# Spectral mixing and Strassen MLP on one core: weight-block sums moved from GpSimd to accumulating DMAs, and a new order of VectorE's work

## The chip, the core and the metric

The kernel runs on one core of one Trainium2 chip. The metric is device time in microseconds (us): the median of three runs of the whole program. The engines are named as in the profile: PE is TensorE (its weight loads are listed apart as PEld), DVE is VectorE, ACT is ScalarE, POOL is GpSimd, SP is SyncE, which issues DMAs.

## What is computed

```python
h  = x + irfft2(rfft2(layernorm(x)) * (w_r + 1j * w_i))       # x: 1 x 2048 x 576
h2 = h + relu(layernorm(h) @ w1) @ w2                         # w1: 576 x 4608, w2: 4608 x 576
```

All inputs and the output are float32. The sizes are S = 2048 tokens, D = 576 and Dff = 4608.

## The kernel before, in words

**Stages.** The two Fourier transforms are done as matrix products with constant tables (forward up to about 65 us, the product with the filter up to about 115 us, the inverse from there on). The inverse transform runs in the loop over t = 0 to 22 near the end of the function: `inv_d(t)` and `inv_a(t)` handle token tile t (16 tiles), `stat2` and `norm2` apply the second layer norm, `sumsx` and `project` transpose the normed tokens and split each number into a high and a low float32r part. Tokens of tiles 0 to 7 land in `T` in SBUF, those of tiles 8 to 15 go through the DRAM tile `Td` and are fetched later.

**The MLP** uses a Strassen-like scheme with seven products instead of eight, in both of its matrix products, and each product is three float32r matmuls (high by high, high by low, low by high). It is cut into NS = 18 steps: steps 0 to 8 serve the first half of the tokens, steps 9 to 17 the second half, and each step handles 512 of the 4608 hidden columns. A step has 14 slots, k = 0 to 13: two units u of seven products m. `slot(S, k)` interleaves two steps: the first matrix product of step S (`mm1`, `evac`) and the second one of step S-1 (`form`, `prod`). Step 0's first product has no partner and is interleaved with the last tiles of the inverse transform (t = 16 to 22); step 17's second product runs alone at the end.

**Weight operands.** For w1, unit v = 2S+u needs 17 blocks of 128 columns in `WF` (high and low): four plain blocks, four sums S1 to S4 of blocks (two 128-row parts each) and the rows 512 to 575. `load1` fetches the plain blocks, `sums1` (L475) forms the sums on GpSimd into the buffer SW, `split1` (L483) makes high and low parts on ACT and DVE in four groups. For w2, `load2` fetches the blocks B11, B12, B21, B22 of a step, `sums2` (L493) forms T1 to T4 on GpSimd, partly in place, and `split2` (L504) makes the seven operands' high and low parts.

**Hidden operands.** `evac` (L541) adds the PSUM tiles X and Y and applies the relu; `hsum` (L513) forms sums of the hidden blocks on DVE; `form` (L520) makes high and low parts of them. `prod` (L555) does 12 matmuls and then adds the PSUM result to the token tile `xs` on DVE (L570).

**Order.** Nothing is reordered by a scheduler: each engine runs its instructions in the order in which the code records them, and semaphores between engines come from the tiles that are read and written. So on GpSimd a sum stands where `tasks_old`, `tasks_new`, `sums1` or the loop over t put it, and everything recorded behind it on GpSimd waits for it: L396 of `inv_d`, L223 to L226 of the layer norm, L423 of `sumsx`. The same holds for SP and its loads. The places of the sums before the change:

```python
if t in (0, 1, 4, 5):
    sums1(t // 4, t % 4)                                  # loop over t
...
if k == 11:
    split2(s, "B11")
    sums2("T1", "T2", "T3")                               # tasks_new
...
if v and k in (3, 5, 9, 12):
    sums1(v + 1, int(k in (5, 12)))
```

The functions that the change touches, as they stood:

## Time and profile before

| | |
|---|---|
| median of 3 runs | 1077.87 us (1076.83 to 1078.52) |
| the profiled execution | 1077.19 us; span of its instructions 1075.4 us |
| granted TensorE clock, mean | 0.99 |
| busy, share of the span | PE 94%, PEld 83%, DVE 86%, ACT 48%, POOL 34% |
| DMA | 85.13 MB, mean 79 GB/s |
| stages | from 243 us to 1043 us steps 1 to 17; before that the transforms and step 0, behind it the last second product |

A profile page counts an engine as busy while an instruction of its executes; a wait is put down to the instruction of another engine that ended it ("<-"). In rows of the timeline the columns are start, duration, engine, line, operation, what is written from what is read, shapes and count, and in brackets the idle time before and its releaser. A line is that of the kernel before; L161 is the helper that all ACT copies go through, L158 that of the transforms' matmuls, L467 the subtraction in `split`.

### The profile page before, as it was taken

Reading aid. Unit: us, or ns where it says so; the run is one execution under the profiler, and the core shown is the slowest. Engines: PE = TensorE matmul, PEld = TensorE weight load, DVE = VectorE, ACT = ScalarE, POOL = GpSimd, SP = SyncE. Lnnn points to the kernel's source line nnn. Section 1 sums busy time; section 2 is a strip of 40 time slices with the busy share of each in tenths; the row PEclk is TensorE's granted clock in tenths of the full one; section 3 lists DMA queues with packets and bytes.
Section 4 is the critical chain, followed back from the end, with each engine's and each line's share of the span. In section 5 each row is a group of like instructions: output and inputs, shape, how many; then the busy total and the mean of one; then the engine's idle time right before and its main releaser. Section 6 shows DMA issues by size and latency. Waiting matters only on the chain.

```text
span 1075.4 us, 16681 instructions
## 1 busy us (share of the span) xinstructions
PE 1011.2 (94%) x6344; PEld 887.4 (83%) x6344; DVE 921.2 (86%) x1367; ACT 514.9 (48%) x904; POOL 368.4 (34%) x384
## 2 busy tenths in 40 slices
PE   8999598779999999999999999999999999999997
PEld 7788476659988988888888989888898988888896
DVE  7587478679899898989989898998989898998987
ACT  4533133556464545545454544545454554545442
POOL 4200166453424252342425235242523424251420
PEclk9999899999999999999999999999999999999999
DMA  8850900563121212112121744212121121212013
GB/s 235 198 133 2 225 1 1 146 183 97 53 67 35 69 36 58 58 44 75 36 69 36 265 147 103 82 36 69 36 58 49 46 82 38 69 30 64 15 31 89
DMA packets 73936, 85.13 MB, mean 79 GB/s; under 512 B 5248, under 2 KB 69248, under 8 KB 72960
## 3 DMA queue, kind: packets, MB, share of 16 engines
q1 hardware_dynamic: 73856, 84.06, 27.7%
q8 instruction: 50, 0.82, 0.3%
q14 instruction: 30, 0.25, 0.1%
HBM read 71.98 MB, written 12.06 MB: 78 GB/s over the span
## 4 chain that ended last, share of the span: by engine, by line
PE 56%; DVE 30%; ACT 7%; issue 3%; DMA 2%; POOL 2%; SPq 1%; POOLq 0%; DVEq 0%; ACTq 0%
PE d L565 22%; PE X L539 15%; PE Y L539 9%; PE d L158 6%; DVE WF L467 6%; DVE e L467 5%; DVE A L570 4%; DVE G L467 3%; DVE h L516 3%; PE dd L158 2%; DVE HF L467 2%; DVE h L552 2%; ACT e L161 1%; ACT WF L161 1%; DVE st L220 1%
## 5 line engine op out<-in xcount | busy, mean ns | idle before, releaser
L539 PE MATMUL X<-T,WF 128*128 128x512 f32 x864 | 230.4, 399 | 12.1 <-DVE WF L467 8.8
L570 DVE TENSOR_TENSOR A<-A,d 128x576 f32<-128x576 f32 x252 | 188.2, 747 | 41.5 <-PE d L565 41.3
L565 PEld LDWEIGHTS d<-e,G 128*128 128x128 f32 x1512 | 213.7, 188 | 11.8 <-issue 1.4
L565 PE MATMUL d<-e,G 128*128 128x288 f32 x1512 | 221.2, 295 | 1.2 <-DVE A L570 1.0
L553 ACT ACTIVATE h<-h 128x512 f32<-128x512 f32 x108 | 68.3, 633 | 315.1 <-DVE h L552 314.7
L481 POOL TENSOR_TENSOR e<-e 128x256 f32<-128x256 f32 (+1 forms) x108 | 98.2, 916 | 300.0 <-DVE WF L467 289.2
L539 PEld LDWEIGHTS X<-T,WF 128*128 128x128 f32 x864 | 154.8, 190 | 44.5 <-DVE WF L467 15.8
L539 PE MATMUL Y<-T,WF 128*128 128x512 f32 x648 | 169.0, 396 | 15.5 <-DVE h L552 15.5
L467 DVE TENSOR_TENSOR WF<-e,WF 128x640 fp32r<-128x640 f32 (+2 forms) x144 | 142.4, 1000 | 32.5 <-ACT WF L161 32.5
L539 PEld LDWEIGHTS Y<-T,WF 128*128 128x128 f32 x648 | 115.4, 188 | 38.6 <-DVE h L552 19.5
L565 PEld LDWEIGHTS d<-e,e 128*128 128x128 f32 x756 | 106.9, 188 | 7.4 <-issue 1.8
L565 PE MATMUL d<-e,e 128*128 128x288 f32 x756 | 110.9, 295 | 1.8 <-DVE A L570 1.6
L565 PEld LDWEIGHTS d<-e,HF 128*128 128x128 f32 x756 | 107.7, 189 | 5.3
L565 PE MATMUL d<-e,HF 128*128 128x288 f32 x756 | 111.2, 296 | 0.0
L497 POOL TENSOR_TENSOR e<-e 128x576 f32<-128x576 f32 x18 | 32.3, 1796 | 229.6 <-DVE e L467 216.9
L467 DVE TENSOR_TENSOR e<-e,e 128x576 fp32r<-128x576 f32 x108 | 96.6, 908 | 15.7 <-ACT e L161 14.4
L516 DVE TENSOR_TENSOR h<-h,h 128x512 f32<-128x512 f32 (+1 forms) x126 | 109.8, 882 | 0.0
L467 DVE TENSOR_TENSOR G<-h,G 128x512 fp32r<-128x512 f32 x126 | 103.6, 823 | 0.1
L161 ACT ACTIVATE WF<-e 128x640 fp32r<-128x640 f32 (+2 forms) x144 | 91.0, 645 | 9.1 <-POOL e L481 9.1
L481 POOL TENSOR_TENSOR e<-e,e 128x256 f32<-128x256 f32 x72 | 82.0, 1139 | 2.8
L161 ACT ACTIVATE u<-X 128x512 f32<-128x512 f32 x72 | 42.5, 590 | 82.4 <-PE X L539 82.3
L161 ACT ACTIVATE G<-h 128x512 fp32r<-128x512 f32 x126 | 77.8, 619 | 6.5 <-DVE h L516 3.5
(103 smaller groups left out, 1296.4 us busy)
## 6 DMA issues: line engine op xcount, KB each, us to landing
e<-in_B_w_dram SPq DMA_DIRECT2D x72, 288.0 KB, 2.9
e<-in_B_w_dram SPq DMA_DIRECT2D x36, 512.0 KB, 3.7
Td<-h SPq DMA_DIRECT2D x28, 256.0 KB, 3.0
T<-Td SPq DMA_DIRECT2D x7, 1024.0 KB, 8.8
A<-in_A_x_dram SPq DMA_DIRECT2D x16, 288.0 KB, 9.2
e<-in_B_w_dram SPq DMA_DIRECT2D x72, 64.0 KB, 3.4
out_dram<-A SPq DMA_DIRECT2D x32, 144.0 KB, 2.5
X<-in_A_x_dram SPq DMA_DIRECT2D x12, 288.0 KB, 7.7
```

Of the source, the lines that this page charges most:

```text
L158: nc.tensor.matmul(o, l, r, start=start, stop=stop)
L161: nc.scalar.activation(o, i, AF.Copy, **kw)
L220: nc.vector.bn_stats(st[:, i, h, :], xs[:, t0 + i, 288 * h:288 * h + 288])
L467: nc.vector.tensor_sub(l, v, h)
L481: (nc.gpsimd.tensor_sub if n_ else nc.gpsimd.tensor_add)(*ops[n_])
L497: nc.gpsimd.tensor_sub(d, a, b)
L516: f(raw(s, d, j), raw(s, a, j), raw(s, b, j))
L539: nc.tensor.matmul(o, l, r, start=first and n_ == 0, stop=n_ == len(ops) - 1, skip_group_check=not first)
L552: nc.vector.tensor_add(h, a, Y)
L553: nc.scalar.activation(h, h, AF.Relu)
L565: nc.tensor.matmul(o[:, tt], f[:, l, j, 128 * tt:128 * tt + 128], w[:, r, j], start=first and n_ == 0, stop=n_ == 5, skip_group_check=not ...
L570: nc.vector.tensor_add(xt, xt, o)
```

## The change

Four things are changed at once.

1. **Sums of w1's blocks.** `sums1` is gone but for one 128-column sum (`rsum`). `wsum(v, step)` builds S1 to S4 in four steps per unit: step 0 is a plain load from SP of the block A21 into four places; steps 1 to 3 are DMAs from GpSimd's queue with `accum_op=ALU.add`, which add A22 to three of them, A11 to three and A12 to one. Each step is two DMAs. SW has two buffers now instead of one, so a unit's sums are started up to two units ahead.
2. **Sums of w2's blocks.** `sums2` is gone. Each operand is loaded by SP from its first block, and the others are added by GpSimd's accumulating DMAs: T2 takes two, T1 and T3 one each, T4 three. B11, B21 and B22 are plain loads. Operands rotate through five buffers.
3. **Signs.** The seven products are turned so that all weight sums are plain sums: S1, S2 and the A22 blocks are split with the factor -1 (on DVE a `scalar_tensor_tensor` in place of the subtraction), two relu evacuations take scale -1, two `hsum`s change sign, and P6 and P7 are subtracted from the tokens instead of added.
4. **Order and buffers.** `total` (the addition to the tokens) is cut out of `prod`; for odd k it stands before `tasks_new`, for even k behind `tasks_late`. Splits are spread over the slots, `hsum` of S2 and S4 is done in one instruction instead of two, `split1` has five groups instead of four. The `Td` stores are issued right behind each split and their staging tiles are apart from the hidden tiles (`HF`, 4 buffers; `h` has 6 instead of 7).

The core of the diff:

```diff
-    def sums1(v, part, only=None):
...
+    def wsum(v, step):
+        fh, kh, a, b = ((1, 0, 0, 4), (1, 1, 0, 3), (0, 0, 1, 4), (0, 1, 2, 3))[step]
+        for k in range(2):
+            src = bass.AP(tensor=w1.tensor, offset=w1.offset + (256 * kh + 128 * k) * 4608 + 256 * (v % 18) + 128 * fh,
+                          ap=[[4608, 128], [0, b - a], [1, 128]])
+            dst = SW[v % 2][:, 4 * k + a:4 * k + b]
+            if step:
+                nc.gpsimd.dma_start(dst, src, accum_op=ALU.add)
+            else:
+                nc.sync.dma_start(dst, src)
...
+    VSUM = {"B11": ("11",), "B21": ("21",), "T2": ("12", "11", "22"), "T1": ("12", "11"), "B22": ("22",),
+            "T3": ("12", "22"), "T4": ("12", "11", "22", "21")}
...
-    def sums2(*names):
...
+    def load2(s, n_, step):
+        u, h = (int(c) - 1 for c in VSUM[n_][step])
         f = 512 * (s % 9) + 256 * u
+        src = w2[f:f + 256, 288 * h:288 * h + 288].rearrange("(j p) d -> p j d", p=128)
+        if step:
+            nc.gpsimd.dma_start(vtile(s, n_), src, accum_op=ALU.add)
+        else:
+            nc.sync.dma_start(vtile(s, n_), src)
...
+    def tasks_late(s, k):
+        if k == 2:
+            hsum(s, "S4")
+        for kk, n_ in ((3, "T1"), (4, "T3"), (5, "B22"), (7, "T4")):
+            if k == kk:
+                split2(s, n_)
+        for kk, step in ((0, 1), (2, 2), (4, 3)):
+            if k == kk:
+                load2(s, "T4", step)
...
+            if m in (1, 3) and v:
+                wsum(v + 1, 2 + m // 2)
+        if v + 2 < 2 * NS:
+            if m == 2:
+                load1(v + 2)
+            if m in (4, 6):
+                wsum(v + 2, m // 2 - 2)
...
             prod(S - 1, k)
             tasks_old(S - 1, k)
+            if k % 2:
+                total(S - 1, k)
         if S < NS:
             tasks_new(S, k)
+        if S:
+            tasks_late(S - 1, k)
+            if k % 2 == 0:
+                total(S - 1, k)
...
-        if t in (0, 1, 4, 5):
-            sums1(t // 4, t % 4)
...
+        if t in (0, 6, 7, 8):
+            wsum(0, max(0, t - 5))
+        if 16 <= t < 20:
+            wsum(1, t - 16)
+        if t == 9:
+            rsum(0)
+        if 8 <= t < 13:
+            split1(0, (0, 1, 2, 4, 3)[t - 8])
```

What this does to GpSimd's queue over one step in the middle of the MLP, before (L481 are sums of w1's blocks, L497 of w2's; the e tiles with numbers 1319 and 1359 hold w1, 1323 the sums, 1958 and 1961 w2):

```order
L481 TENSOR_TENSOR e_1323<-e_1319 128x256
L481 TENSOR_TENSOR e_1323<-e_1323,e_1319 128x256
L497 TENSOR_TENSOR e_1958<-e_1958 128x576
L497 TENSOR_TENSOR T_300_1857<-e_1961,e_1958 128x576
L497 TENSOR_TENSOR e_1958<-e_1961,e_1958 128x576
L481 TENSOR_TENSOR e_1323<-e_1319 128x256
L481 TENSOR_TENSOR e_1323<-e_1319,e_1323 128x256
L481 TENSOR_TENSOR e_1323<-e_1319 128x128
L481 TENSOR_TENSOR e_1323<-e_1359 128x256
L481 TENSOR_TENSOR e_1323<-e_1323,e_1359 128x256
L497 TENSOR_TENSOR e_1961<-e_1961,T_300_1857 128x576
```

And the same queue after, about one unit and a half (L486 is `wsum`, L516 `load2`, L492 `rsum`; e_1323 and e_1848 are the two SW buffers, e_1915, e_1967 and V_1860 hold w2's sums, in_B_w_dram is w1 or w2 in DRAM):

```order
L492 TENSOR_TENSOR e_1323<-e_1319 128x128
L516 DMA e_1915<-in_B_w_dram 128x2x288
L486 DMA e_1848<-in_B_w_dram 128x3x128 x2
L516 DMA e_1915<-in_B_w_dram 128x2x288
L486 DMA e_1848<-in_B_w_dram 128x128 x2
L516 DMA e_1915<-in_B_w_dram 128x2x288
L486 DMA e_1323<-in_B_w_dram 128x3x128 x2
L516 DMA e_1967<-in_B_w_dram 128x2x288
L492 TENSOR_TENSOR e_1848<-e_1356 128x128
L486 DMA e_1323<-in_B_w_dram 128x3x128 x2
```

The sums that read SBUF are gone but for L492; in their place stand DMA issues, each of which adds into a tile that the DMA before it on that tile must have finished.

At the start of the inverse transform GpSimd's queue began like this before (L396 belongs to `inv_d` of tiles 0, 1 and 2):

```order
L396 TENSOR_TENSOR e_1313<-e_1313 128x287
L481 TENSOR_TENSOR e_1323<-e_1319 128x256
L481 TENSOR_TENSOR e_1323<-e_1323,e_1319 128x256
L396 TENSOR_TENSOR e_1333<-e_1333 128x287
L481 TENSOR_TENSOR e_1323<-e_1319 128x256
```

It begins like this after:

```order
L396 TENSOR_TENSOR e_1313<-e_1313 128x287
L396 TENSOR_TENSOR e_1333<-e_1333 128x287
L396 TENSOR_TENSOR e_1350<-e_1350 128x287
L396 TENSOR_TENSOR e_1371<-e_1371 128x287
L396 TENSOR_TENSOR e_1394<-e_1394 128x287
```

The sums of unit 0 no longer stand between the first tiles; its accumulating DMAs come at t = 6, 7 and 8.

On DVE, slots 1 and 2 of a step read like this before (L552 is the evacuation of Y at m = 1, L570 the addition to the tokens, L516 halves of the hidden sums S2 and S4, L467 the subtraction of a split; T_300 holds w2's T2, e_1323 w1's sums, A is `xs`; the last two rows are of slot 3):

```order
L552 TENSOR_TENSOR h_3047<-s_296_1847,Y 128x512
L570 TENSOR_TENSOR A_1284<-A_1284,d_2217 128x2x288
L516 TENSOR_TENSOR h_2651<-h_2732,h_2651 128x512
L467 TENSOR_TENSOR e_2065<-T_300_1857,e_2065 128x576
L467 TENSOR_TENSOR HF_1856<-h_2651,HF_1856 128x512
L570 TENSOR_TENSOR A_1284<-A_1284,d_2216 128x2x288
L516 TENSOR_TENSOR h_2851<-h_2851,h_2651 128x512
L467 TENSOR_TENSOR WF_1288<-e_1323,WF_1288 128x640
L467 TENSOR_TENSOR e_2112<-h_2732,e_2112 128x512
L570 TENSOR_TENSOR A_1284<-A_1284,d_2217 128x2x288
```

The same slots of a later step read like this after (L571 is that evacuation, L535 a whole hidden sum, L595 the addition to the tokens, L471 the subtraction of `split`, HF a hidden operand's form; the last four rows are of slot 3):

```order
L571 TENSOR_TENSOR h_3928<-s_297_1851,Y 128x512
L535 TENSOR_TENSOR h_3516<-h_3603,h_3516 128x1024
L595 TENSOR_TENSOR A_1284<-A_1284,d_2242 128x2x288
L471 TENSOR_TENSOR HF_2182<-h_3516,HF_2182 128x512
L471 TENSOR_TENSOR WF_1288<-e_1323,WF_1288 128x2x256
L535 TENSOR_TENSOR h_3722<-h_3722,h_3516 128x1024
L595 TENSOR_TENSOR A_1284<-A_1284,d_2241 128x2x288
L471 TENSOR_TENSOR HF_2183<-h_3603,HF_2183 128x512
L595 TENSOR_TENSOR A_1284<-A_1284,d_2242 128x2x288
L471 TENSOR_TENSOR WF_1288<-e_1323,WF_1288 128x128
L471 TENSOR_TENSOR e_2234<-e_1915,e_2234 128x576
```

The split of T2 has left these slots (it stands in slot 11 of the step before). The split of w1's sums S3 and S4 (WF, 2x256) stands ahead of the hidden sum S4 and of slot 2's addition to the tokens, where it stood behind both, and its 128 columns of rows 512 to 575 follow in slot 3.

More of the change, by code (lines that the diff above doesn't have):

```diff
@@ L473, in load1 @@
             nc.sync.dma_start(t[64 * h:64 * h + 64, 4], w1[512:576, f])
-    def sums1(v, part, only=None):
-        t, S = V1[v % 2], M["SW"]
-        A11, A12, A21, A22 = (t[:, 2 * k:2 * k + 2, 128 * f:128 * f + 128] for f, k in ((0, 0), (0, 1), (1, 0), (1, 1)))
-        S1, S2, S3, S4 = (S[:, 2 * i:2 * i + 2] for i in range(4))
-        ops = ((S1, A21, A22), (S2, S1, A11), (S3, A11, A21), (S4, A12, S2), (S[:, 8], t[:, 4, :128], t[:, 4, 128:]))
-        for n_ in ((0, 1), (2, 3, 4))[part] if only is None else [only]:
-            (nc.gpsimd.tensor_sub if n_ else nc.gpsimd.tensor_add)(*ops[n_])
@@ new lines, in rsum @@
+    def rsum(v):
+        t = V1[v % 2]
+        nc.gpsimd.tensor_add(SW[v % 2][:, 8], t[:, 4, :128], t[:, 4, 128:])
+    def split1(v, g):
+        t, S = V1[v % 2], SW[v % 2]
+        if g in (2, 3):
+            h, l = (WF[:, i, 8:16].rearrange("p (k s) f -> p k s f", k=2)[:, :, 2 * g - 4:2 * g - 2] for i in range(2))
+            split(h, l, S[:, 0:8].rearrange("p (k s) f -> p k s f", k=2)[:, :, 2 * g - 4:2 * g - 2], g == 2)
+        else:
+            a, b, src = {0: (0, 5, t[:, :, :128]), 1: (5, 8, t[:, 2:5, 128:]), 4: (16, 17, S[:, 8:9])}[g]
+            split(WF[:, 0, a:b], WF[:, 1, a:b], src, g == 1)
@@ L530, in mm1 @@
         for k in range(2):
-            w = [WF[:, i, BLOCK[a] + k] for i in range(2)]
+            w = [WF[:, i, BLOCK[a] + k * (4 if a[0] == 'S' else 1)] for i in range(2)]
             t = [T[:, b, i, k] for i in range(2)]
@@ L692 @@
         VF.append(ebuf([128, 1152], F32R).rearrange("p (a j d) -> p a j d", a=2, j=2))
[L693 to L694 removed]
+    split2(0, "T2")
+    load2(0, "T4", 0)
+    HF += [sb([128, 2, 2, 256], "HF", 4, F32R, "mid") for _ in range(2)]
     M["c0"], M["c1"] = (ps(), ps()), ps()
```

136 lines of the change are left out of this document (55 added, 81 removed).

## Prediction

> **What bounds the kernel now.** I read the page first, then the waits and busy times of the long middle stage, then single stalls in the timeline.
>
> ```profile
> PE 1011.2 (94%) x6344; PEld 887.4 (83%) x6344; DVE 921.2 (86%) x1367; ACT 514.9 (48%) x904; POOL 368.4 (34%) x384
> ```
>
> TensorE is busy 94% of the 1075.4 us span; it can only be helped by taking its waits away. Steps 1 to 17 (from 243 to 1043 us) in the busy times by stretch, whose columns are PE, PEld, DVE, ACT, POOL, granted clock, DMA share and GB/s, and TensorE's waits there:
>
> ```profile
> 243.10:1043.40 800.30, 778.80 (x4551) 696.44 (x4550) 723.79 (x950) 404.05 (x731) 279.81 (x233) 1.00 0.22 66
> PE Y L539 <- DVE h L552: 12.7, 16, 0.9
> PE X L539 <- DVE WF L467: 8.8, 16, 0.6
> ```
>
> A step takes 800.3 / 17 = 47.1 us, of which TensorE works 778.8 / 17 = 45.8. The difference, 21.5 us in all, is two stalls per step, both on VectorE. Why VectorE is late there shows in the timeline of one step, VectorE, GpSimd and TensorE:
>
> ```profile
> 710.13 1.68 DVE L467 TENSOR_TENSOR e<-e,e 128x576 fp32r<-128x576 f32 x1
> 711.73 1.92 DVE L467 TENSOR_TENSOR WF<-e,WF 128x512 fp32r<-128x512 f32 x1
> 717.99 1.92 DVE L467 TENSOR_TENSOR G<-h,G 128x512 fp32r<-128x512 f32 x1
> 721.71 0.68 DVE L467 TENSOR_TENSOR G<-h,G 128x512 fp32r<-128x512 f32 x1
> 724.25 0.76 DVE L467 TENSOR_TENSOR e<-T,e 128x576 fp32r<-128x576 f32 x1
> 709.76 1.43 POOL L497 TENSOR_TENSOR T<-e,e 128x576 f32<-128x576 f32 x1
> 711.14 1.95 POOL L497 TENSOR_TENSOR e<-e,e 128x576 f32<-128x576 f32 x1
> 723.03 1.66 PE L539 MATMUL Y<-T,WF 128*128 128x512 f32 x6 [0.76 <-DVE h L552]
> ```
>
> The same 128x512 subtraction takes 1.92 us while GpSimd adds blocks and 0.68 us when it does not, a 128x576 one 1.68 and 0.76 us. Grouped by line and shape over the stage (the count, then busy us and mean ns):
>
> ```profile
> L467 DVE TENSOR_TENSOR G<-h,G 128x512 fp32r<-128x512 f32 x120 | 99.5, 829 | 0.0
> L467 DVE TENSOR_TENSOR WF<-e,WF 128x512 fp32r<-128x512 f32 x33 | 42.5, 1286 | 9.5 <-ACT WF L161 9.5
> L570 DVE TENSOR_TENSOR A<-A,d 128x576 f32<-128x576 f32 x237 | 177.0, 747 | 39.7 <-PE d L565 39.6
> ```
>
> Against 0.68 us the first two groups alone lose 120 x 0.15 + 33 x 0.61 = 38 us on VectorE, 2.2 us a step, and VectorE stands still for 800.3 - 723.8 = 76.5 us besides. So VectorE has time enough over a step; it is late only behind GpSimd's sums.
>
> Ahead of that stage, one stall stands out, at the start of the inverse transform (GpSimd, then TensorE):
>
> ```profile
> 131.53 0.72 POOL L481 TENSOR_TENSOR e<-e 128x256 f32<-128x256 f32 x1 [10.80 <-DMA e<-in_B_w_dram]
> 133.02 0.69 POOL L396 TENSOR_TENSOR e<-e 128x287 f32<-128x287 f32 x1
> 133.77 1.32 PE L158 MATMUL dd<-e,cc 128*128 128x288 f32 x2 [9.77 <-POOL e L396]
> ```
>
> GpSimd waits 10.8 us for the first w1 load, because the sum of unit 0 stands ahead of tile 1's L396; TensorE waits 9.8 us for that.
>
> **The change part by part.** The sum is made on the profiled execution, 1077.19 us (span 1075.4 and 1.8 around it); it lies 0.7 us under the median, so the same forecast serves for both.
>
> *Start of the inverse transform.* The queue on GpSimd now has the L396 of tiles 0 to 4 in a row, and no load stands ahead of them. The whole 9.8 us can go. What comes back: the five splits of unit 0 on VectorE are moved to t = 8 to 12, where a projection is split too, and three accumulating pairs plus L492 stand ahead of the layer norm and `sumsx` at t = 6 to 9. Unit 0's splits cost VectorE 4.3 us before:
>
> ```profile
> 133.75 1.19 DVE L467 TENSOR_TENSOR WF<-e,WF 128x512 fp32r<-128x512 f32 x1 [8.33 <-ACT WF L161]
> 140.66 2.05 DVE L467 TENSOR_TENSOR WF<-e,WF 128x640 fp32r<-128x640 f32 x2
> 145.57 1.05 DVE L467 TENSOR_TENSOR WF<-e,WF 128x384 fp32r<-128x384 f32 x1
> ```
>
> They will again, at the new place, and of the DMA issues each may hold `sumsx` by 1 to 2 us. I take -7, between -10 and -3.
>
> *Steps 1 to 17: GpSimd's sums.* 279.8 us of GpSimd work, and with it the stretch of VectorE, goes but for two 128-column sums a step. In the step shown, VectorE reaches the evacuation that TensorE waits for after losing about 0.9 + 1.2 + 1.2 us in the three stretched rows alone, for a wait of 0.76 us. Half of that gain would be enough. The second wait (0.6 us, for the split of S3 and S4) is also met by the new order, which puts that split ahead of a hidden sum and an addition to the tokens. Nothing else waits on TensorE in this stage, so what is late next is TensorE itself, 45.8 us a step. All of it would be -21.5; I take -18, as some slots are now full of splits, and -12 at the weak end.
>
> *The same stage: new work.* The turned signs add four `scalar_tensor_tensor` a step, which the trace does not show; between the quiet 0.68 us of a 128x512 row and the 1.92 us of a stretched one, 0 to 5 us a step, covered by VectorE's 76.5 / 17 = 4.5 us of idle time and the 2.2 us and more that it gains. The fifth split group costs under 0.7 us per unit, in the same cover. I take nothing for both.
>
> GpSimd's queue gets 19 DMA issues a step (12 for w1, 7 for w2). The trace has none; the nearest rows are SP's issue of such a load and the longest GpSimd instruction (the third row prices the two sums that stay, 0.9 us at most):
>
> ```profile
> 694.61 0.37 SPq L471 DMA_DIRECT2D e<-in_B_w_dram  x1
> L497 POOL TENSOR_TENSOR e<-e,e 128x576 f32<-128x576 f32 x17 | 33.1, 1947 | 0.0
> L481 POOL TENSOR_TENSOR e<-e 128x256 f32<-128x256 f32 (+1 forms) x99 | 91.4, 930 | 289.2 <-DVE WF L467 289.2
> ```
>
> That is 7 to 37 us a step, under 45.8 at both ends; I take the middle, about 1.2 us each or 23 us. Each of these DMAs also waits until the DMA before it on its tile has landed, and everything behind it on GpSimd waits too. The steps of one sum stand two slots apart (2 x 3.3 us), and the last one three slots, 9.8 us, ahead of its split. A plain load lands within that:
>
> ```profile
> e<-in_B_w_dram SPq DMA_DIRECT2D x72, 288.0 KB, 2.9
> e<-in_B_w_dram SPq DMA_DIRECT2D x36, 512.0 KB, 3.7
> e<-in_B_w_dram SPq DMA_DIRECT2D x72, 64.0 KB, 3.4
> T<-Td SPq DMA_DIRECT2D x7, 1024.0 KB, 8.8
> 200.00:243.10 43.10, 32.51 (x158) 25.99 (x157) 28.95 (x43) 25.46 (x46) 22.60 (x29) 0.94 0.70 202
> ```
>
> Bytes: a step loads plainly 7 x 288 KB of w2, 4 x 256 KB of w1's step 0 and 1280 KB of w1's blocks, 4.42 MB, where it was 2.5; and it adds 7 x 288 + 8 x 192 + 4 x 64 KB, 3.90 MB. The last row moves 202 GB/s at a DMA share of 0.70, so 289 GB/s would fill the engines: 15.3 us a step for the plain loads, and 13.5 us for the adding ones if they went at the same rate. That is 28.8 of 45.8 us. The rate of an adding DMA is in no row; bounds are this rate and, on the far side, the third rival. I take that the engines have room.
>
> The Trainium skill speaks against this: "Collectives: The Full Stack", under the bandwidth ceiling, says that a DMA that adds must read two sources through one ring and measured 1.93 times slower than a copy. No run here shows it yet; by it the adding loads would take 26 us, and the sum 41 of 45.8 us, still under TensorE's time, with no room for a burst.
>
> *Steps 8 and 9.* Seven `T<-Td` loads of 1 MB are issued within seven slots, and the page shows that slice already at 265 GB/s:
>
> ```profile
> DMA  8850900563121212112121744212121121212013
> GB/s 235 198 133 2 225 1 1 146 183 97 53 67 35 69 36 58 58 44 75 36 69 36 265 147 103 82 36 69 36 58 49 46 82 38 69 30 64 15 31 89
> ```
>
> 7.34 MB take 25.4 us at 289 GB/s, and half a step's 28.8 us comes on top: 40 us of transfers in 23 us of time, on SP's queue in a row. Loads fall 17 us behind with a lead of 9.8: between 0 and +12 once. I take +4, as part of that queue has a longer lead (T1, T3 and T itself are needed six slots later or more).
>
> *Step 0* (200 to 243 us). Three L497 stand there ahead of the last `sumsx`:
>
> ```profile
> PE d L434 <- POOL e L423: 4.4, 1, 4.4
> ```
>
> They go, but three DMA issues with waits of their own stand in their place: -4 to +4, I take 0.
>
> *The end* (32 us). VectorE bounds it:
>
> ```profile
> 1043.40:1075.40 32.00, 24.20 (x170) 22.61 (x168) 26.15 (x40) 10.31 (x18) 2.30 (x2) 0.97 0.32 75
> ```
>
> Two hidden sums become one instruction each, under 1 us; T4's three additions in a row, some 4 us each from the landing times above, must fit between step 17's slot 12 and slot 7 of the last product, about 15 us. -1 to +5, I take +1.
>
> Sum: 1077.2 - 7 - 18 + 0 + 4 + 0 + 1 = 1057.2 us.
>
> **The rivals.**
>
> *VectorE stays stretched, or new waits take the old ones' place.* If a DMA issue on GpSimd holds VectorE as a sum does, 19 issues of 1.2 us, 23 us a step, stand where 279.8 / 17 = 16.5 us of sums stood, and the stalls stay. Or a late sum holds a split, and with it VectorE, about as long. For it: nothing in the trace tells a sum's reading from GpSimd being busy. Against: additions to the tokens (L570), which read PSUM, average 0.75 us, so it is a matter of what is read, and an issue reads no tile. Only the start is then gained, and perhaps 5 us of the stalls: 1077.2 - 7 - 5 + 4 + 1 = 1070, from 1062 to 1083. The Trainium skill's "SBUF — State Buffer", on who interferes with whom, says that a VectorE instruction with two SBUF inputs contends with a GpSimd instruction that reads SBUF and not with one that only writes it; the stretched rows agree with its first half, and by its second half this rival falls.
>
> *The DMA engines become the bound: slower.* Place: every step from 1 to 17. With the plain loads at 15.3 us, a step has 30.5 us for its 3.90 MB of adding. The gain of the forecast outside this stage is 2 to 3 us, so the kernel is slower once a step passes about 47.2 us: 31.9 us of adding, 122 GB/s, 0.42 of the plain rate. At a third of the plain rate a step takes 15.3 + 40.5 = 55.8 us, +8.7 x 17 = +148, about 1220; at 0.38 it takes 50.8, about 1138. Speaks for it: 512-byte pieces and a read of the target. Against: the stage's mean share is 0.22 today.
>
> *GpSimd's issuing becomes the bound: slower.* 19 issues and two sums of 0.9 us pass 47.2 us from 2.4 us per issue; at 2.7 us a step takes 53.1, +6.0 x 17 = +102, about 1175. Against: that is over the longest GpSimd row of the trace. For: waits for landing stand in the same queue, and these count with the issue.
>
> **How the numbers follow.** Forecast 0.55, stretched or replaced waits 0.15, DMA engines 0.17, GpSimd's issuing 0.13. The forecast's own range is 1040 (every term at its good end: -10 - 21.5 - 4 - 1) to 1070. The range for all reaches up to 1110, where the two slow rivals begin to bind; they lie above it in about 0.17 of the cases, and 0.03 lie below. A difference of 0.2% (2.2 us) is about what can be told from no change. Faster: 0.53 of the forecast and 0.10 of the first rival, 0.63. Same: 0.06, from the edges of all. Slower: nearly all of the two slow rivals and 0.02 of the first, 0.31.
>
> **What would show it.** Right: TensorE starts tile 1's transform without the 9.8 us wait; the two waits per step shrink to under a fifth; 128x512 subtractions average under 0.72 us; a step takes 46 us; GpSimd's queue is idle a third of the time. Wrong: waits of DVE or ACT on DMA in every step (the engines or the issuing bound), a DMA share over 0.9, steps of 48 us and more; or subtractions that stay over 0.8 us beside GpSimd's issues.

## The result, and the profile after

The changed kernel takes 1613.1 us (median) against 1078.1 us for the kernel before on the same chip: a ratio of 1.495, with an interval from 1.492 to 1.499. The forecast was 1057 us, with a range up to 1110.

The first profile of it is of an execution of 1717.3 us at a granted TensorE clock of 0.588; the rows below are of a further one, of 1613.6 us at 0.835, and a step is nearly as long in both (76.8 and 76.4 us), so that 93 of the 104 us between them lie ahead of step 1.

The page of the changed kernel: span, busy times, DMA queues (q0 is GpSimd's, q1 is SP's) and the chain that ended last.

```profile
span 1611.8 us, 17577 instructions
...
PE 1161.7 (72%) x6344; PEld 1001.4 (62%) x6344; DVE 823.3 (51%) x1367; ACT 521.7 (32%) x940; POOL 492.7 (31%) x510
...
q0 software_dynamic: 102240, 70.21, 34.0%
q1 hardware_dynamic: 126560, 118.87, 25.9%
...
issue 51%; POOL 21%; DVE 9%; PE 7%; DMA 7%; ACT 4%; SPq 0%; POOLq 0%; ACTq 0%; DVEq 0%
```

No engine is near its limit: TensorE fell from 94% to 72%, VectorE from 86% to 51%, and the two DMA queues together keep the DMA engines busy 60% of the time. The chain says "issue", which is time in which an engine waited for nothing that the profile shows, and behind it GpSimd.

Steps 1 to 17, from the first matmul of the second product at 280.3 us to 1578.2, in the busy times by stretch (columns as before: PE, PEld, DVE, ACT, POOL, granted clock, DMA share, GB/s). This row and the rows of this stage in the kernels below end at the start of the last 12 matmuls of step 17's slots, 1.4 to 1.6 us earlier than the row of the kernel before; where that matters, the time to the same point as before is given.

```profile
280.30:1578.20 1297.90, 923.08 (x4540) 804.69 (x4539) 629.13 (x950) 409.36 (x763) 390.84 (x351) 0.82 0.61 115
```

That is 1297.9 / 17 = 76.3 us a step (76.4 to the same point as before, 1579.8 us) where it was 47.1. The difference of the spans, 536 us, is made up of 499 us here and 37 us ahead of step 1 (280.3 against 243.2); the end takes 32.0 us in both. GpSimd in the same stretch, grouped by line and operation (count, busy us, mean ns, then the idle time ahead of them and what ended it):

```profile
L486 POOL DMA_DIRECT2D e<-in_B_w_dram x198 | 245.9, 1242 | 617.9 <-issue 557.1 <-DVE h L571 54.7 <-DVE WF L471 4.0
L516 POOL DMA_DIRECT2D e<-in_B_w_dram x95 | 119.5, 1258 | 226.5 <-issue 221.9 <-DMA e<-in_B_w_dram 4.5
L492 POOL TENSOR_TENSOR e<-e 128x128 f32<-128x128 f32 x34 | 32.2, 947 | 0.0
L516 POOL DMA_DIRECT2D V<-in_B_w_dram x24 | 30.3, 1261 | 64.8 <-issue 61.1 <-DMA V<-in_B_w_dram 3.7
```

GpSimd is busy for 390.8 of the 1297.9 us, and idle ahead of its DMA issues for 617.9 + 226.5 + 64.8 = 909.2: together all of the stretch. Its queue is full with waiting. Of the idle time 840.1 us carry the name "issue". There are 317 issues, so each holds the queue for (390.8 - 32.2 + 840.1) / 317 = 3.78 us: about 1.13 of work (1.24 by the rows, which overlap a little) and 2.65 of waiting. The timeline of GpSimd shows them one by one (start, duration, and in brackets the idle time before):

```profile
936.21 1.22 POOL L516 DMA_DIRECT2D e<-in_B_w_dram  x1 [2.96 <-issue]
936.97 1.40 POOL L486 DMA_DIRECT2D e<-in_B_w_dram  x1
941.15 0.86 POOL L486 DMA_DIRECT2D e<-in_B_w_dram  x1 [2.78 <-issue]
941.73 1.52 POOL L516 DMA_DIRECT2D e<-in_B_w_dram  x1
947.15 1.29 POOL L486 DMA_DIRECT2D e<-in_B_w_dram  x1 [3.90 <-issue]
952.55 1.29 POOL L486 DMA_DIRECT2D e<-in_B_w_dram  x1 [4.11 <-issue]
```

The last two are the halves k = 0 and 1 of one `wsum` step. They write different columns of the tile and no semaphore stands between them, and still the second starts 5.4 us after the first: 0.36 us after the last landing signal of the first, at 952.19 us. It is so throughout the stage. Of the some 250 issues that waited under "issue", nine in ten start 0.25 to 0.36 us after the last landing signal of an earlier DMA of GpSimd's, whatever tile that one wrote. A 192 KB adding DMA never starts while another is in flight (144 of 144 in the whole execution), and two are in flight together only where one is of 64 KB. So the wait is for an earlier DMA to land, but not through a semaphore of the same tile, which the prediction had looked at. How lateness travels from there, in the waits of VectorE, ScalarE and TensorE over the same stretch (us in total, times, longest):

```profile
DVE e L471 <- ACT e L161: 366.3, 84, 17.1
...
ACT e L161 <- DMA e<-in_B_w_dram: 279.4, 27, 16.3
...
ACT WF L161 <- POOL e L492: 170.3, 32, 8.0
...
PE X L558 <- ACT h L567: 124.1, 16, 11.7
PE Y L558 <- DVE h L571: 112.4, 18, 7.3
```

The splits of weight operands wait on ScalarE for a transfer that GpSimd has issued late, VectorE waits behind them, and TensorE behind its evacuations. The stretched subtractions have gone all the same. VectorE's group of the split in `form` (L471 on `HF`, which was L467 on `G`):

```profile
L471 DVE TENSOR_TENSOR HF<-h,HF 128x512 fp32r<-128x512 f32 x238 | 164.6, 692 | 5.8 <-ACT HF L161 4.1
```

692 ns, where it was 829 (825 over the three groups that this one replaces), beside 317 DMA issues of GpSimd.

Two explanations were set against each other first. One: GpSimd's issue waits for room for the DMAs' descriptors, whose store the kernel sizes with `dynamic_dma_scratch_size=1024` where it is set up. Its rival: the adding itself is slow, in the DMA engines or because each DMA must see the one before it land.

### The profile page after: what moved, and what is told of

It is laid out like the page before. It is cut to its first block, busy times and chain, and to the rows that moved or that the text cites. A ratio compares the mean times of both kernels' runs of the same rounds, so it can differ in the third digit from the quotient of the medians.

```text
span 1715.5 us, 17577 instructions
## 1 busy us (share of the span) xinstructions
PE 1558.9 (91%) x6344; PEld 1178.8 (69%) x6344; DVE 829.2 (48%) x1367; ACT 530.7 (31%) x940; POOL 497.2 (29%) x510
## 3 DMA queue, kind: packets, MB, share of 16 engines
q0 software_dynamic: 102240, 70.21, 31.8%
## 4 chain that ended last, share of the span: by engine, by line
PE 46%; issue 31%; POOL 13%; DMA 4%; DVE 3%; ACT 2%; POOLq 0%; ACTq 0%; DVEq 0%
PE d L584 15%; PE d L158 11%; POOL e L486 8%; PE X L558 8%; PE Y L558 7%; PE dd L158 3%; DMA e<-in_B_w_dram 3%; POOL e L516 2%; PE d L287 1%; DVE A L595 1%; ACT e L161 1%; DMA V<-in_B_w_dram 1%; POOL e L492 1%; PE d L434 1%; DVE HF L471 1%
## 5 line engine op out<-in xcount | busy, mean ns | idle before, releaser
L584 PEld LDWEIGHTS d<-e,HF 128*128 128x128 f32 x3024 | 592.8, 223 | 85.9 <-issue 24.7
L584 PE MATMUL d<-e,HF 128*128 128x288 f32 x3024 | 646.2, 384 | 0.1
L486 POOL DMA_DIRECT2D e<-in_B_w_dram x216 | 267.7, 1242 | 640.4 <-issue 561.2
L558 PE MATMUL X<-T,WF 128*128 128x512 f32 x864 | 343.7, 555 | 90.9 <-ACT h L567 67.1
L558 PE MATMUL Y<-T,WF 128*128 128x512 f32 x648 | 254.7, 549 | 29.9 <-DVE h L571 29.9
L595 DVE TENSOR_TENSOR A<-A,d 128x576 f32<-128x576 f32 x252 | 188.8, 749 | 171.8 <-PE d L584 171.3
L516 POOL DMA_DIRECT2D e<-in_B_w_dram x99 | 124.4, 1257 | 248.1 <-issue 242.9
L471 DVE TENSOR_TENSOR e<-e,e 128x576 fp32r<-128x576 f32 x100 | 75.5, 755 | 243.9 <-ACT e L161 243.9
L471 DVE TENSOR_TENSOR HF<-h,HF 128x512 fp32r<-128x512 f32 x252 | 173.3, 688 | 4.1 <-ACT HF L161 3.4
L161 ACT ACTIVATE HF<-h 128x512 fp32r<-128x512 f32 x252 | 155.7, 618 | 24.1 <-DVE h L535 13.3
L161 ACT ACTIVATE WF<-e 128x512 fp32r<-128x512 f32 (+3 forms) x180 | 100.3, 557 | 177.9 <-POOL e L492 142.8
L471 DVE TENSOR_TENSOR WF<-e,WF 128x512 fp32r<-128x512 f32 (+2 forms) x108 | 66.4, 615 | 139.7 <-ACT WF L161 139.7
L558 PE MATMUL Y<-R,WF 128*128 128x512 f32 x216 | 98.1, 546 | 0.0
L535 DVE TENSOR_TENSOR h<-h,h 128x1024 f32<-128x1024 f32 (+1 forms) x90 | 92.4, 1026 | 0.0
L468 DVE SCALAR_TENSOR_TENSOR WF<-e,WF 128x512 fp32r<-128x512 f32 (+1 forms) x72 | 45.8, 635 | 68.6 <-ACT WF L161 68.6
L396 POOL TENSOR_TENSOR e<-e 128x287 f32<-128x287 f32 x16 | 14.1, 883 | 178.7 <-DVE e L394 176.5
```

The costliest lines, as they stand in the source:

```text
L161: nc.scalar.activation(o, i, AF.Copy, **kw)
L468: nc.vector.scalar_tensor_tensor(l, v, -1.0, h, op0=ALU.mult, op1=ALU.subtract)
L471: nc.vector.tensor_sub(l, v, h)
L486: nc.gpsimd.dma_start(dst, src, accum_op=ALU.add)
L516: nc.gpsimd.dma_start(vtile(s, n_), src, accum_op=ALU.add)
L535: f(raw(s, d, j), raw(s, a, j), raw(s, b, j))
```

## Experiments on the room for descriptors

**Twice the room, nothing else.**

```diff
-    nc = _bacc.Bacc("TRN2", target_bir_lowering=False, num_devices=1, dynamic_dma_scratch_size=1024)
+    nc = _bacc.Bacc("TRN2", target_bir_lowering=False, num_devices=1, dynamic_dma_scratch_size=2048)
```

> The changed kernel with 2048 instead of 1024 bytes per partition set aside for GpSimd's DMA descriptors; nothing else. Theory R (GpSimd's issue waits for room for descriptors: with 1024 bytes about one 192 or 288 KB DMA is in flight, so 19 issues a step come about 4.2 us apart, 80 us a step): twice the room lets two be in flight, issues come 2.1 to 2.5 us apart, a step takes 46 to 50 us, the whole 1050 to 1110 us. Rival S (the semaphore waits of one addition for the one before it set the pace): no change, 1600 to 1620 us. Rival D (the DMA engines are slow at adding): no change, within 2%.

Measured: 1082.0 us, ratio to before 1.0057 (1.0029 to 1.0084). One number at the set-up takes 531 of the 535 us away, though all 19 adding DMAs of a step and their bytes stay. GpSimd in steps 1 to 17 of this kernel:

```profile
L486 POOL DMA_DIRECT2D e<-in_B_w_dram x197 | 250.2, 1330 | 220.8 <-issue 167.4 <-DMA e<-in_B_w_dram 35.5 <-DVE HF L471 8.4
L516 POOL DMA_DIRECT2D e<-in_B_w_dram x95 | 122.9, 1337 | 141.7 <-issue 75.7 <-DMA e<-in_B_w_dram 57.9 <-DMA T<-Td 7.1
```

The waits on "issue" are down from 779 us in these two groups to 243, and not yet gone. Two adding DMAs of 192 or 288 KB are now in flight at once, which never happened at 1024.

**Four times the room.** The kernel's other buffers had to be narrowed a little for the space; a run further below has the narrow buffers at 1024, and is slow, so the narrowing is not what helps.

```diff
-EW = 1344
+EW = 1284
...
-    nc = _bacc.Bacc("TRN2", target_bir_lowering=False, num_devices=1, dynamic_dma_scratch_size=1024)
+    nc = _bacc.Bacc("TRN2", target_bir_lowering=False, num_devices=1, dynamic_dma_scratch_size=4096)
```

> The changed kernel with 4096 bytes for GpSimd's DMA descriptors, and EW 1284 instead of 1344 (smaller e buffers, the largest use is 1282) to make room for it. Theory R: four DMAs in flight, issues as close as their own 1.25 us allow, a step at TensorE's 45.8 us, the whole 1040 to 1070 us. Rival S: 1600 to 1620 us. Rival D: adding moves 70.2 MB at 31.8% of the engines in the changed kernel, 129 GB/s; if that is their limit a step needs 15.3 us for plain loads and 30.3 us for adding, so about as long as TensorE; 1060 to 1120 us, with a DMA share over 0.9 and little difference from 2048 bytes.

Measured: 1056.9 us, ratio 0.982 (0.980 to 0.983). The span and the two DMA queues on its page:

```profile
span 1054.1 us, 17577 instructions
...
q0 software_dynamic: 102240, 70.21, 49.5%
q1 hardware_dynamic: 126560, 118.87, 40.5%
```

GpSimd's timeline at about the same place of the stage:

```profile
943.28 0.90 POOL L486 DMA_DIRECT2D e<-in_B_w_dram  x1 [2.41 <-DMA e<-in_B_w_dram]
945.95 0.86 POOL L486 DMA_DIRECT2D e<-in_B_w_dram  x1 [1.78 <-DMA e<-in_B_w_dram]
947.56 1.20 POOL L516 DMA_DIRECT2D e<-in_B_w_dram  x1 [0.75 <-DMA e<-in_B_w_dram]
948.76 2.67 POOL L486 DMA_DIRECT2D e<-in_B_w_dram  x2
954.02 1.20 POOL L516 DMA_DIRECT2D e<-in_B_w_dram  x1 [2.60 <-DMA e<-in_B_w_dram]
```

Now two issues go out back to back ("x2", 2.67 us), and where GpSimd waits in these rows it is for the landing of an earlier DMA on the same tile. Those waits are there in every step and hardly reach TensorE: from 245.4 to 1024.3 us a step takes 45.8 us, of which TensorE is idle for 0.3. That the room held the adding DMAs back is shown. What the store holds isn't seen in the profile; the Trainium skill, "DMA: Bandwidth & Descriptors", section "SWDGE vs HWDGE vs iDMA", says that GpSimd writes a DMA's descriptors into rings in a part of SBUF set aside for that, from which the DMA engines drain them. The three times at 1024, 2048 and 4096 agree with it; no run shows how many descriptors fit.

**The same transfers without the addition,** at 1024. This kernel leaves the forming of the sums out: the last block loaded takes the place of the sum.

```diff
             if step:
-                nc.gpsimd.dma_start(dst, src, accum_op=ALU.add)
+                nc.gpsimd.dma_start(dst, src)
...
-            nc.gpsimd.dma_start(vtile(s, n_), src, accum_op=ALU.add)
+            nc.gpsimd.dma_start(vtile(s, n_), src)
```

> The changed kernel (1024 bytes) with the additions left out of GpSimd's DMAs: the same 19 a step, same sizes and order, plain copies; the sums are not formed. Theory R: a copy drains faster than an addition, so issues come 3 to 3.5 us apart instead of 4.2 and a step takes 60 to 70 us: 1300 to 1450 us, still far above before. Rival D (it is the adding itself): a step falls to about 46 us, 1040 to 1080 us. Rival S: the waits stand as they were and landings come about 1 us earlier, 1400 to 1550 us.

Measured: 1041.0 us, ratio 0.967 (0.964 to 0.969). The two queues on this kernel's page:

```profile
q1 hardware_dynamic: 126560, 118.87, 40.0%
q0 software_dynamic: 21600, 70.21, 22.8%
```

GpSimd's DMA issues in it from 245 to 1022 us, grouped as above (a third, smaller group is left out):

```profile
L486 POOL DMA_DIRECT2D e<-in_B_w_dram x196 | 136.3, 696 | 239.0 <-DMA e<-in_B_w_dram 91.9 <-issue 63.4 <-DVE HF L471 22.1
L516 POOL DMA_DIRECT2D e<-in_B_w_dram x95 | 68.8, 725 | 208.7 <-DMA e<-in_B_w_dram 190.9 <-issue 17.8
```

The same 70.21 MB go in 21600 packets instead of 102240, an issue takes 0.70 to 0.73 us instead of 1.24, and the small room is hardly felt: 81 us of waits on "issue" in these two groups. The theory of the room had expected 1300 to 1450 us here and was wrong in that: 1041 us lies where the rival of the slow addition had it, a rival that for its part had expected no change from more room. So neither holds alone: the room is too small for DMAs that add, and not for the same DMAs without the addition. The trace shows that these take less of it: two copies of 192 KB, or two of 288 and one of 64 KB, are in flight at once at 1024. The addition thus costs three things: a longer issue, more of the room, and the rate. For the rate: 70.21 MB take 22.8% of 1037.0 us = 236 us of the 16 engines, 297 GB/s; with the addition (in the kernel with 4096) 49.5% of 1054.1 = 522 us, 135 GB/s, 2.2 times slower. The prediction's rule from "Collectives: The Full Stack" of the Trainium skill (1.93 times, measured there between two collectives) was near, and the value taken in the sum (no slower than a plain load) was wrong.

**No DMA on GpSimd at all.** The adding DMAs are left out, and so the sums are never formed.

```diff
             if step:
-                nc.gpsimd.dma_start(dst, src, accum_op=ALU.add)
+                pass
...
-            nc.gpsimd.dma_start(vtile(s, n_), src, accum_op=ALU.add)
+            pass
```

> The changed kernel without any DMA from GpSimd (the additions are left out, so the sums are not formed); all else, the loads from SP, the signs and the new order of VectorE's work, stays. All theories: this is the floor of the new order with no sums at all. If VectorE's order and the freed GpSimd are worth what the prediction said, a step takes 45.8 to 46.1 us, the start loses its 9.8 us stall, and the whole comes to 1040 to 1055 us with a granted clock of 0.99. If the new order itself costs time, it stays over 1060 us.

Measured: 1036.5 us, ratio 0.962 (0.958 to 0.966), a little below what was expected. This is the floor of the new order, with sums that cost nothing: 41 us under the kernel before, which shows what hiding the sums could give at best. Its two executions took 1033.3 and 1039.6 us, so the floor is known to some 3 us.

**The old order without GpSimd's sums.** In the kernel before, the sums are left out and plain blocks are split in their place.

```diff
-            (nc.gpsimd.tensor_sub if n_ else nc.gpsimd.tensor_add)(*ops[n_])
+            pass
...
-            nc.gpsimd.tensor_sub(d, a, b)
+            pass
```

> The kernel before with all weight sums on GpSimd left out (the splits read plain blocks in their place, so the output is not the reference's); its order, signs and loads stay. Theory C (GpSimd's sums, by stretching VectorE, make both stalls of a step; the order of VectorE's work is worth nothing more): both stalls go and the 9.8 us stall at the start goes, 1040 to 1052 us, within 1% of the changed kernel without additions (1036 us). Rival O (the new order is needed for the stall on the splits of S3 and S4): one stall of about 0.5 us a step stays, 1055 to 1062 us.

Measured: 1039.2 us, ratio 0.965 (0.962 to 0.967). The old order is within 3 us of the new one's floor once GpSimd's sums are gone, which these runs can't tell from no difference. So no gain from the new order of VectorE's work, by itself, is shown; nearly all of the possible gain is the sums' absence from GpSimd.

## Experiments on how many sums to move

**w1's sums as additions on GpSimd, w2's by adding DMAs,** at 1024: 7 adding DMAs a step instead of 19.

```diff
     def wsum(v, step):
-            if step:
-                nc.gpsimd.dma_start(dst, src, accum_op=ALU.add)
...
+        for d, a, b in ((), ((S1, A21, A22),), ((S2, S1, A11), (S3, A21, A11)), ((S4, S2, A12),))[step]:
+            nc.gpsimd.tensor_add(d, a, b)
```

> The changed kernel (1024 bytes for descriptors) with w1's sums formed by GpSimd as plain sums from the loaded blocks, in the places of the additions; w2's sums stay adding DMAs, 7 a step instead of 19. Theory R (room for descriptors sets the pace of the issues, about 4.9 us for 288 KB): 7 x 4.9 = 34 us a step, under TensorE's 45.8, so no collapse: 1040 to 1070 us, the upper part if GpSimd's sums still stretch VectorE enough to stall TensorE. Rival A (any adding DMA in this kernel costs its latency): above 1200 us.

Measured: 1066.3 us, ratio 0.990 (0.987 to 0.993): 1% under the kernel before, with the room as it was. Part of the stretch on VectorE comes back with the sums: the 128x512 subtraction of `form` takes 766 ns on the mean, where it took 692. Steps 1 to 17 are as long as in the kernel before (47.0 us a step); the gain lies ahead of them (6 us) and at the end (2 us).

**T4 on GpSimd, room 4096.** T4 = T2 + B21 is formed by one addition in place of a load and three adding DMAs: 16 a step.

```diff
+    def sum4(s):
+        nc.gpsimd.tensor_add(vtile(s, "T4"), vtile(s, "T2"), vtile(s, "B21"))
...
-        for kk, step in ((0, 1), (2, 2), (4, 3)):
-            if k == kk:
-                load2(s, "T4", step)
...
+        if k == 12 and s:
+            sum4(s)
```

> The changed kernel with 4096 bytes for descriptors, and T4 formed by one GpSimd addition of T2 and B21 in place, instead of a load and three adding DMAs: 16 adding DMAs a step, 3.02 MB of adding instead of 3.90. With 4096 bytes the DMA engines are at a share of 1.0, adding at 135 GB/s. If the engines are what is left of the loss (1057 against 1036 us without additions): 22.5 + 15 = 37 us of 45.8 a step, 1038 to 1047 us. If instead the waits of one addition for the other are: little change, 1052 to 1058 us.

Measured: 1053.2 us, ratio 0.977 (0.975 to 0.979). That is in the range of little change: relieving the DMA engines in steps 1 to 17 (a share of 0.86 from 245 to 600 us, where it was 1.01) is not what was missing. Step 1 starts at 246.9 us, no earlier than with 19 (245.4).

**S4 on GpSimd as well:** 12 adding DMAs a step, of 128 KB instead of 192 for two of them in three.

```diff
+        if step == 3:
+            S = SW[v % 2][:, 0:8].rearrange("p (k s) f -> p k s f", k=2)
+            nc.gpsimd.tensor_add(S[:, :, 3], S[:, :, 1], V1[v % 2][:, 2:4, :128])
+            return
```

> As the run with T4 on GpSimd, and S4 of w1 also formed by one GpSimd addition per unit (of S2 and A12) instead of its share of the adding DMAs: 12 adding DMAs a step, 2.2 MB. Engines: 16.5 + 14 = 31 us a step. Against it stands GpSimd's reading beside VectorE, some 2 us more a step. 1038 to 1046 us: within 0.4% of the run with T4 alone if the engines have room already there, slower than it by more if GpSimd's stretching counts.

Measured: 1046.9 us, ratio 0.972 (0.970 to 0.974), the fastest version that forms all the sums: 30 us under the kernel before and 10 us above the floor. It is 0.6% faster than with T4 alone, which neither branch of the expectation had. The gain is ahead of step 1, which starts at 239.5 us; a step takes 45.6 us in both.

**The same with 2048 and with 1024,** which asks whether the room or the number of DMAs is what counts. The edit for 2048 is shown; that for 1024 differs in the number alone.

```diff
-    nc = _bacc.Bacc("TRN2", target_bir_lowering=False, num_devices=1, dynamic_dma_scratch_size=4096)
+    nc = _bacc.Bacc("TRN2", target_bir_lowering=False, num_devices=1, dynamic_dma_scratch_size=2048)
```

> The best version so far (T4 and S4 formed on GpSimd, 12 adding DMAs per step instead of 19), but with 2048 bytes of room for descriptors instead of 4096. With 19 adding DMAs, 2048 bytes cost 25 us against 4096 (1082.0 and 1056.9). If the cost of the smaller room is a wait per adding DMA that only shows where GpSimd's queue is full, 12 per step leave slack and the time is 1046 to 1052 us. If the smaller room holds the transfers themselves back (fewer of them at a time, a lower rate), about 12/19 of the 25 us stays: 1060 to 1065 us.

> The best version (T4 and S4 formed on GpSimd, 12 adding DMAs per step), with the 1024 bytes of room for descriptors that the change has. If each adding DMA holds GpSimd's queue for some 3.9 us there (1.25 us of issue and 2.7 us of waiting, as worked out from the changed kernel's profile), 12 of them take 47 us a step, and the four to five sums of 7 us in all lie beside them in part: 47 to 54 us a step where the version with more room takes 45.7, so 1046.9 + 17 x (1.3 to 8) = 1069 to 1185 us, with waits of GpSimd on issue of some 30 us a step. Rival: the smaller room costs only what all 19 need at once, and 12 fit without waiting: under 1055 us.

Measured with 2048: 1047.2 us, ratio 0.971 (0.970 to 0.973), the same as with 4096, as the first branch had it. With 1024: 1262.6 us, ratio 1.173 (1.167 to 1.179), more than the 1185 us that the expectation ended at. Steps 1 to 17 with 1024, GpSimd's DMA issues (L490 is `wsum`, L520 `load2`):

```profile
L490 POOL DMA_DIRECT2D e<-in_B_w_dram x132 | 160.5, 1216 | 361.0 <-issue 312.6 <-DVE A L602 19.9 <-DVE WF L468 13.6
L520 POOL DMA_DIRECT2D e<-in_B_w_dram x53 | 64.6, 1219 | 185.1 <-issue 181.2 <-DMA e<-in_B_w_dram 3.9
...
L520 POOL DMA_DIRECT2D V<-in_B_w_dram x15 | 18.2, 1214 | 48.1 <-issue 44.5 <-DMA V<-in_B_w_dram 3.6
```

And the busy times of that stretch:

```profile
270.00:1227.80 957.80, 812.04 (x4541) 718.83 (x4540) 651.65 (x948) 408.29 (x763) 319.26 (x285) 0.92 0.58 117
```

GpSimd's sums take 108 us of its 319.3, so an issue costs (319.3 - 108 + 538.3) / 200 = 3.75 us, the price found above (3.78). 11.8 of them make 44 us a step, and the sums, 6.4 us, and GpSimd's other waits, 6 us, come on top: 56.3 us a step, where the expectation had thought that the sums would lie beside the waits in part. The rest of its miss lies ahead of step 1, which starts at 270.0 us and not at 239.5. The price per issue holds over these two kernels, where GpSimd's queue is the bound. In the kernel with 7 adding DMAs a step it isn't, and there an issue held the queue for 2.56 us (146.0 us of issues and 161.5 of waits on "issue" over 120 of them), 18 us a step, which fits beside GpSimd's sums.

**Where the last 10 to 20 us lie.** In the kernel with 4096, the transfers of the tokens' projections are left out, so the second half of the rows comes from the first half's projections.

```diff
-                nc.sync.dma_start(Td[f0 + f, :, :, i % 4], ...)
+                0 and nc.sync.dma_start(Td[f0 + f, :, :, i % 4], ...)
...
-            nc.sync.dma_start(T[:, b]..., Td[b]...)
+            0 and nc.sync.dma_start(T[:, b]..., Td[b]...)
```

> The kernel after the change with 4096 bytes of room for descriptors, and without the projections of tokens 1024 to 2047: neither their 28 stores to Td nor the seven 1 MB loads of T at steps 8 and 9 are issued, so the second half of the rows is computed from the first half's projections. All 19 adding DMAs per step stay. Theory D: what is left of the loss against the version without adding DMAs (1056.9 against 1036.5 us) lies mostly in step 0, where the stores, the plain loads and the adding DMAs together fill the DMA engines (TensorE works 29.1 us of the 45 from 200 to 245 us, against 35.4 without adding DMAs); then TensorE is busy for 33 us or more of that stretch and the time falls to 1042 to 1050 us. Rival R: an adding DMA is late there by its own two or three waits in GpSimd's queue, whatever else the DMA engines carry: TensorE stays at 29 to 31 us of the 45, and the time at 1053 to 1058 us.

Measured: 1038.9 us, ratio 0.964 (0.962 to 0.965): below the expected 1042 to 1050, with all 19 adding DMAs in place. From 200 to 245 us TensorE is busy for 33.6 us, as theory D had it. The busy times by stretch in step 0, in the steps behind it, and around steps 8 and 9, with 4096:

```profile
195.00:245.00 50.00, 33.43 (x138) 25.98 (x137) 21.36 (x37) 23.48 (x42) 30.86 (x36) 0.83 1.12 249
245.00:600.00 355.00, 352.55 (x2069) 319.44 (x2068) 294.85 (x440) 191.37 (x356) 190.11 (x167) 0.99 1.01 191
600.00:760.00 160.00, 157.08 (x919) 141.75 (x918) 128.37 (x193) 81.35 (x151) 79.73 (x71) 0.99 1.09 234
```

The same without the transfers of `Td`:

```profile
195.00:245.00 50.00, 38.02 (x190) 30.05 (x188) 30.38 (x51) 28.21 (x52) 35.35 (x40) 0.97 0.71 119
245.00:600.00 355.00, 355.00 (x2101) 321.71 (x2102) 297.96 (x443) 192.85 (x359) 190.93 (x170) 1.00 1.01 188
600.00:760.00 160.00, 160.00 (x949) 145.09 (x949) 132.86 (x198) 86.20 (x161) 86.18 (x76) 1.00 1.05 201
```

The numbers in brackets are the matmuls done in each stretch. With the `Td` transfers TensorE does 52, 32 and 30 fewer; at 160.00 / 949 = 0.169 us each these 114 are 19 us, which is the difference of the two kernels (18.0 us). So some 9 us lie in step 0, where the stores, the plain loads and the adding DMAs come together at a share of 1.12, 5 in the steps behind it, and 5 where the 1 MB loads of T come on top. In the last two stretches only about half of that is idle time of TensorE (2.5 and 2.9 us); for the rest its matmuls took longer (0.170 to 0.171 us each instead of 0.169). Where nothing but weights moves, a share of 1.01 costs TensorE nothing (355.00 of 355).

The kernel without adding DMAs keeps the `Td` transfers, so it shows what they cost by themselves. Step 1 starts at 229.5 us in it, at 235.7 without the `Td` transfers and at 245.4 with both. So of the 16 us lost ahead of step 1 against that floor, 10 go with the `Td` transfers and 6 stay with the adding DMAs alone: theory D has the larger part, and rival R is not ruled out for the smaller. That the whole time comes within 2.4 us of the floor's median is partly chance: in steps 1 to 17 the same matmuls kept TensorE busy for 768.5 us here and for 774.6 in the profiled execution of the floor, for which no run shows a cause. Whether the order of the stores, their staging tiles or the bytes themselves decide was not tried apart.

**The changed kernel once more,** to see whether TensorE's clock sets the length of a step.

> The changed kernel itself once more, for a profile of an execution of about 1613 us (the profile at hand is of one of 1717 us, with a granted TensorE clock of 0.588). If GpSimd's queue sets the length of a step, its issues and their waits again fill the step (19 issues at about 3.7 us, 71 us a step); if a good part of the step is TensorE's own slow clock, GpSimd shows waits on other engines of 10 us a step and more.

Measured: 1613.6 us in one execution; its rows are those of the section on the result. GpSimd's queue fills a step at both clocks, and its waits on other engines are 69 / 17 = 4 us a step. The expectation had 71 us for the issues, and they take 317 / 17 x 3.78 = 70.5; with the two sums and the other waits a step is 76.4 us, against 76.8 at the lower clock, so TensorE's clock does not set the step.

## Why the prediction was wrong, point by point

**The step that failed is the price of GpSimd's 19 DMA issues.** The prediction took "about 1.2 us each or 23 us" a step, from SP's issue and the longest GpSimd row, and a queue of 45.8 us with room. The instruction itself was met: 1.24 us. What was missing is the wait ahead of it, 2.65 us at this room, until an earlier DMA of GpSimd's has landed; it raises the price to 3.78 us and the queue to 76.4 us a step. No row of the trace of before could show it, because GpSimd issued no DMA there. The bounds did not hold it either: with 7 to 37 us the dear end was called under TensorE's time, and 70 us came.

**The third rival is the one that came true**, with its place (every step) and its turning point: issues dearer than 2.4 us. Its price, 2.7 us and 1175 us, was too low, and its mechanism was only near the one that acted. It counted waits for the landing of the DMA before on the same tile; with 4096 those waits are there and cost little. What held the queue at 1024 was the landing of whichever DMA had the room. Against it stood that 2.4 us "is over the longest GpSimd row", which speaks of what an instruction works and says nothing of what it waits for. The condition itself was right and a chance of 0.13 was too small for it: of an operation that an engine has never done in the trace, the cost was bounded by operations of another kind.

**The DMA engines** (second rival) did not become the bound: their share is 0.61. With room for the descriptors they came near it. The adding loads went at 135 GB/s, so 3.90 MB take 29 us a step against the 31.9 from which that rival decides, and the share is 1.01. The forecast's 13.5 us was wrong by a factor of two, and without effect, except in step 0 and in steps 8 and 9.

**The stretch on VectorE** (first rival) went, as forecast: 692 ns for the 128x512 split. The rule of the Trainium skill's "SBUF — State Buffer", on who interferes with whom, is borne out: a GpSimd that issues DMAs does not slow it as one that adds tiles did.

**The gain of steps 1 to 17** was right in kind and too small. With 4096 the stage takes 778.9 us instead of 800.2, counted to the same point, -21.4 us, where the prediction had -18 for the stalls and +4 for steps 8 and 9. TensorE is idle for 5.4 us in it, where it was for 21.5: 16 us of the gain. The other 5 us are the same 4551 matmuls, which kept it busy for 773.5 us instead of 778.7; the prediction had held these at 45.8 us a step, and why they are shorter stays open. Steps 8 and 9 cost some 5 (the 30 matmuls above).

**The start and step 0** were forecast at -7 and 0, and came to +2.2 with 4096 together (step 1 starts at 245.4 us instead of 243.2). The wait of 9.8 us did go: TensorE's longest wait on L396 is 1.9 us there. But as much and more was lost behind it, the larger part to the crowd of transfers that the run without `Td` shows; the prediction had looked there at GpSimd's queue alone, though the busy times by stretch already gave a DMA share of 0.70 for it. In the kernel as changed, this stretch lost 37 us: `sumsx` (L423) stands behind the DMA issues. TensorE's waits on it from 120 to 300 us, where it was 4.4 us before:

```profile
PE d L434 <- POOL e L423: 37.0, 6, 13.3
```

**The end** was forecast at +1, between -1 and +5. Counted from the same point, it takes 29.9 us with 4096 instead of 32.0, -2.1, so T4's three additions held nothing up there.

That the kernel with 4096 comes out at 1056.9 us, where 1057 was forecast, is thus partly chance: its parts are +2.2, -21.4 and -2.1, not -7, -14 and +1.

## What to carry to other kernels

Work that goes from an engine's arithmetic into DMAs issued by GpSimd has a price that no profile of the arithmetic shows: how many of these DMAs may be in flight. Before such a change, look at what the kernel sets aside for their descriptors, and after it at the "issue" waits of GpSimd's groups; two independent DMAs that start a landing time apart are the sign. Spread a kernel's sums over the adding DMAs and the engine by what each has room for: 12 adding DMAs and a few sums on GpSimd did better here than 19 or 16, all three with room, better than 7, which were tried at 1024 alone, and better than none, as in the kernel before.

## What the runs showed of the hardware

- A DMA that adds, issued by GpSimd, takes 1.24 us to issue at 1024 (1.33 at 2048) and a plain one of the same shape 0.70 to 0.73 us; it moves 135 GB/s and not 297, in 102240 packets and not 21600 for the same 70.21 MB.
- At a descriptor store of 1024, an adding issue of 64 to 288 KB held GpSimd's queue for 3.75 to 3.78 us on the mean whether 19 or 12 of them stood in a step. The wait ends some 0.32 us after an earlier DMA of GpSimd's has landed; no two of 128 KB or more were in flight at once. At 2048 the waits on "issue" in the two groups of e tiles fell from 779 to 243 us, and at 4096 to a few us.
- A DMA share of 1.01 over 355 us, in the kernel without `Td`, left TensorE without a wait; a share is no measure of lateness by itself.
- The granted TensorE clock was 0.99 in the kernel before and 0.84 in the changed kernel, where TensorE waits a part of each step, and 0.59 in its first profile. A step was nearly as long at both of the latter (76.4 and 76.8 us). Why the clock was lower was not tried.
